# Two decode layers over a cached K and V: the next pair's keys ahead of a pair's values, a shorter row chain, two filler heads

## The chip, the cores and the metric

The kernel runs on one core of one Trainium2 chip (trn2). The metric is the device time of that core in microseconds (us), the median over runs. Three numbers recur, so they get names. The **item** is one of the eight batch rows. **x1** is the moment when an item's first attention is complete and the row chain starts. **Lateness** is how much later than 2.49 us each 1 MB cache load landed after the one before it, summed; 2.49 us is their spacing while the queue is full.

## The reference, cut to what matters

```python
x = A_x                                        # [8, 1, 448]
x = x + A_ref(layernorm(x), k_cache, v_cache, wq, wo)
x = x + B_ref(layernorm(x), w1, w2, w3, w4)
x = x + A_ref(layernorm(x), k_cache, v_cache, wq, wo)   # the same cache again
x = x + B_ref(layernorm(x), w1, w2, w3, w4)

# A_ref: 16 query heads on 8 key/value heads, Sk = 4096, Dh = 256, softmax over Sk, then wo
# B_ref: h = gelu(layernorm(x) @ w1), shifted along a sequence of one token: hs is zero
#        x1 = x + hs;  return x1 + gelu(layernorm(x1) @ w3) @ w4          # F = 1792
```

With one token per sequence, B_ref is two layer norms in a row and one MLP with gelu in its tanh form. Each cache entry is used twice, by layer 1 and by layer 2, and a row's layer 2 can't start before its layer 1 and the row's MLP are done.

## The kernel before

One item has 8 heads in each of 2 layers: 16 **pairs** (a layer and a head). A pair needs 2 MB of keys and 2 MB of values, in four halves of 1 MB. There are 15 half slots in on-chip memory. The keys of five heads (ten halves) and one value half are kept from layer 1 to layer 2; the others are loaded twice. So an item loads 64 - 11 = 53 halves. The keys arrive as rows and are transposed on TensorE (16 transposes per half), copied back by VectorE or ScalarE, and multiplied: per pair 64 small matmuls for the scores, 64 for the values, 20 for the output projection.

The program builds a list of operations with priorities; a planner with assumed durations puts them in a fixed order on each engine.

```python
HALVES = 15; KEEP_K = 5; KEEP_V = 1; REP = 24
...
    def schedule(self):                        # list scheduler, one queue per engine
        ...
            if e == "sp":                      # a DMA issue
                free[e] = t + 0.45
                start = max(t + 1.0, dma_end)  # assumed latency of a load
                dma_end = start + o.dur
            else:
                end = free[e] = t + (o.dur[e] if isinstance(o.dur, dict) else o.dur)
...
    def mlp(src, skey, n, b0):                 # the row chain
        layernorm(src, skey, n, [("full", xnT[:, :, 0:n], "xnT")])
        layernorm(xnT[:, :, 0:n], "xnT", n, [("split", None, None)])
        ...                                    # 56 matmuls, gelu by exp on VectorE and ScalarE, 70 matmuls
...
    def pair(layer, b, h, kept_k, kept_v, keep_k, keep_v):
        for j in range(2):                     # keys: load, transpose, scores
            if ks[j] is None:
                ks[j] = load_half(A_k_cache, b, h, j)
            ...
            for qd in range(2):
                def sc(t, j=j, qd=qd, s_=ks[j]):
                    for s in range(8 * qd, 8 * qd + 8):
                        i = 16 * j + s
                        for c in range(2):
                            a = slot_ap(s_, s * 256, 256)
                            last = t.matmul(ps[:, 2 * i:2 * i + 2 * REP], a[:, c:256:2],
                                            bcast(rhs(c), REP, 1), start=(c == 0), stop=(c == 1))
                    return last
        ...                                    # max over partitions, exp, sum
        for j in range(2):                     # values: load and multiply, at once
            if vs[j] is None:
                vs[j] = load_half(A_v_cache, b, h, j)
            ...                                # 32 matmuls per half, then 20 with wo
...
    for b in range(B):
        if b + 1 < B:
            fill = lambda: layer1(b + 1, free_heads)    # 3 filler heads while the chain runs
        else:
            fill = lambda: layer2(b - 1, free_heads)
        mid(b, l2_heads[0], l2_heads + free_heads)      # x1 -> norms, MLP, norm -> new queries
        fill()
        layer2(b, l2_heads)                             # the five heads with kept keys
        if b != B - 2:
            layer2(b, free_heads)
        if b + 1 < B:
            layer1(b + 1, kept_heads)                   # keeps ten halves of keys again
```

At x1 ten slots hold kept keys and one a kept value half. Only four slots circulate until the row chain has made the new queries.

## Time and profile before

| | before |
|---|---|
| time, median of 3 runs | 1298.9 us (1296.33 to 1300.52) |
| TensorE busy | 1013.1 us, 78% |
| bytes over the load queue | 455.19 MB |
| lateness, mean of seven items | 22.2 us (18.6 to 25.4) |
| x1 to first new query, mean | 31.6 us |
| last cache load landed, then to the end | 1265.6 us, then 34.9 us |

The page of the kernel before: the span, each engine's busy time, then in 40 slices of the span the granted TensorE clock, the DMA share and the GB/s, and last the queues.

```profile
span 1300.5 us, 52136 instructions
PE 1013.1 (78%) x24217; PEld 963.1 (74%) x24217; DVE 523.1 (40%) x1804; ACT 214.4 (16%) x743; POOL 97.7 (8%) x270
...
PEclk8789889988899887998899988999899888997886
...
GB/s 357 413 399 383 276 399 417 417 256 340 409 418 387 262 334 419 416 331 303 370 417 416 284 292 367 417 416 295 315 409 417 405 252 317 413 390 240 371 365 2
...
q1 hardware_dynamic: 68192, 455.19, 89.4%
q8 instruction: 190, 3.11, 1.0%
```

The queue runs at 416 to 418 GB/s and dips eight times, once per item. What SyncE, which issues the loads, waited for (columns: line, what it waited for, us in total, times, longest us):

```profile
SPq L372 <- PE psS L632: 720.3, 201, 10.4
SPq L372 <- PE psS L594: 228.8, 90, 4.7
```

A load waits for a slot, and a slot comes free by the value matmuls (L632) or the score matmuls (L594) that read it. What TensorE waited for, same columns:

```profile
PE psS L632 <- ACT pT L614: 71.4, 77, 1.6
PE psS L594 <- issue: 45.1, 29, 3.9
PE psT L680 <- DMA kv<-in_A_k_cache_dram: 44.3, 19, 4.2
PE psS L632 <- issue: 36.4, 26, 3.3
...
PE psW L655 <- issue: 14.5, 8, 3.3
```

TensorE waited 71.4 us for the softmax of ScalarE (L614) and 44.3 us for keys. The lines with "issue" are time in which it waited for nothing that the profile shows: 102.0 us in 70 pauses over the whole run.

One item's end, in windows of 10 us around x1 = 433.8. Columns: window, busy us (instructions) of PE, PEld, DVE, ACT and POOL after the window's length, granted clock, DMA share, GB/s.

```profile
393.80:403.80 10.00, 8.10 (x182) 7.38 (x181) 4.82 (x12) 1.81 (x7) 0.75 (x2) 1.00 1.01 416
423.80:433.80 10.00, 8.44 (x166) 7.97 (x163) 4.34 (x13) 1.23 (x5) 0.75 (x2) 0.83 0.54 189
433.80:443.80 10.00, 7.19 (x99) 6.89 (x97) 5.33 (x28) 2.40 (x7) 0.75 (x2) 0.67 0.62 211
```

The load queue falls to half at x1. The timeline just before it (start, us, engine, line, operation, and in brackets the idle time and what ended it):

```profile
424.31 0.56 PE L594 MATMUL psS<-q1T,kv 128*128 128x48 bf16 x16 [0.39 <-DVE kv L688]
...
426.52 0.57 PE L632 MATMUL psS<-pT,kv 128*128 128x48 bf16 x16 [1.17 <-ACT pT L614]
...
438.50 1.97 PE L680 MATMUL psT<-ident_f,kv 128*128 128x128 f32 x8 [2.33 <-DMA kv<-in_A_k_cache_dram]
```

The last pair's scores ended at 424.9 and its value matmuls could start only at 426.5, after the softmax, though the values had landed at 419.8. Twelve microseconds later TensorE sat waiting for keys that had been issued late.

### The profile page before, as it was taken

What the parts mean: (1) busy time and instruction counts of PE and PEld (TensorE: products, weight loads), DVE (VectorE), ACT (ScalarE), POOL (GpSimd) and SP (SyncE); (2) the same over time, 40 slices, a digit from 0 to 9 for tenths busy, and PEclk for the clock granted to TensorE, in tenths of its full rate; (3) what the DMA queues carried; (4) which work ended last, traced back from release to release, by engine and by line L of the source; (5) the groups of instructions that cost most, each with busy time, mean ns of one, the idle gap of its engine ahead of it and who ended that gap; (6) DMA issues with size and microseconds to landing.
All of it is one profiled execution on the core that took longest, in us unless ns stands there. A gap on an engine that the chain in (4) does not pass through costs nothing.

```text
span 1300.5 us, 52136 instructions
## 1 busy us (share of the span) xinstructions
PE 1013.1 (78%) x24217; PEld 963.1 (74%) x24217; DVE 523.1 (40%) x1804; ACT 214.4 (16%) x743; POOL 97.7 (8%) x270
## 2 busy tenths in 40 slices
PE   5767868887788787888688787888778878778784
PEld 4766868877687777777677786877767868778774
DVE  2334414453244522446144541445324453344234
ACT  1112102111111111221011110212111111121110
POOL 0000000000000000000100000000010000000100
PEclk8789889988899887998899988999899888997886
DMA  9999799979999799988999789998899978996980
GB/s 357 413 399 383 276 399 417 417 256 340 409 418 387 262 334 419 416 331 303 370 417 416 284 292 367 417 416 295 315 409 417 405 252 317 413 390 240 371 365 2
DMA packets 68408, 458.52 MB, mean 353 GB/s; under 512 B 6992, under 2 KB 13024, under 8 KB 13536
## 3 DMA queue, kind: packets, MB, share of 16 engines
q1 hardware_dynamic: 68192, 455.19, 89.4%
q8 instruction: 190, 3.11, 1.0%
q14 instruction: 26, 0.21, 0.0%
HBM read 455.15 MB, written 0.01 MB: 350 GB/s over the span
## 4 chain that ended last, share of the span: by engine, by line
PE 63%; DMA 14%; issue 10%; DVE 6%; ACT 4%; SPq 2%; POOL 2%
PE psT L680 22%; PE psS L632 17%; PE psS L594 14%; DMA kv<-in_A_k_cache_dram 12%; PE psW L655 5%; ACT pT L614 3%; DMA kv<-in_A_v_cache_dram 3%; DVE kv L688 2%; PE psC L491 2%; SPq L372 2%; POOL gm L606 2%; DVE pm L604 1%; PE psC L541 1%; DVE nb L608 1%; ACT kv L689 0%
## 5 line engine op out<-in xcount | busy, mean ns | idle before, releaser
L680 PE MATMUL psT<-ident_f,kv 128*128 128x128 f32 x2816 | 448.3, 299 | 46.0 <-DMA kv<-in_A_k_cache_dram 44.3
L688 DVE COPY kv<-psT 128x512 f32<-128x512 f32 x483 | 333.0, 690 | 294.6 <-PE psT L680 291.5
L632 PE MATMUL psS<-pT,kv 128*128 128x48 bf16 x8192 | 300.3, 190 | 110.8 <-ACT pT L614 71.4
L632 PEld LDWEIGHTS psS<-pT,kv 128*128 128x128 bf16 x8192 | 277.1, 101 | 132.4 <-ACT pT L614 85.9
L680 PEld LDWEIGHTS psT<-ident_f,kv 128*128 128x128 f32 x2816 | 332.2, 152 | 48.7 <-DMA kv<-in_A_k_cache_dram 46.3
L689 ACT COPY kv<-psT 128x512 f32<-128x512 f32 x221 | 129.4, 586 | 678.7 <-PE psT L680 678.7
L594 PE MATMUL psS<-q2T,kv 128*128 128x48 bf16 x4096 | 149.8, 192 | 48.1 <-issue 42.9
L594 PEld LDWEIGHTS psS<-q2T,kv 128*128 128x128 bf16 x4096 | 136.4, 102 | 51.6 <-issue 46.1
L594 PE MATMUL psS<-q1T,kv 128*128 128x48 bf16 x4096 | 145.7, 184 | 25.6 <-DVE kv L688 17.5
L594 PEld LDWEIGHTS psS<-q1T,kv 128*128 128x128 bf16 x4096 | 126.7, 97 | 38.6 <-issue 27.1
L614 ACT ACTIVATE pT<-psS,nb 128x32 bf16<-128x32 f32 x256 | 72.8, 294 | 372.4 <-DVE nb L608 372.1
L606 POOL PARTITION_ALL_REDUCE gm<-pm x128 | 45.4, 355 | 1050.2 <-DVE pm L604 1027.9
L655 PE MATMUL psW<-oT,wo_sb 128*128 128x24 bf16 x2560 | 89.9, 183 | 18.2 <-issue 14.5
L655 PEld LDWEIGHTS psW<-oT,wo_sb 128*128 128x128 bf16 x2560 | 83.6, 97 | 23.1 <-issue 20.2
L604 DVE TENSOR_REDUCE pm<-psS 128x2 f32<-128x64 f32 x128 | 28.6, 224 | 132.2 <-PE psS L594 131.9
L644 DVE TENSOR_TENSOR oT<-psS,rc 128x4 bf16<-128x4 f32 x128 | 20.2, 158 | 109.8 <-PE psS L632 109.6
L619 POOL PARTITION_ALL_REDUCE Db<-rs x128 | 51.9, 405 | 117.7 <-ACT pT L614 117.7
L614 ACT ACTIVATION_READ_ACCUMULATOR pT<-psS,nb 128x1 f32 x256 | 50.3, 196 | 0.0
L621 DVE RECIPROCAL rc<-Db 128x2 f32<-128x2 f32 x128 | 20.9, 164 | 66.5 <-POOL Db L619 66.5
L491 PE MATMUL psC<-yb,wq_sb 128*128 128x16 bf16 (+1 forms) x864 | 38.6, 175 | 6.8 <-issue 4.4
L608 DVE TENSOR_SCALAR nb<-gm 128x2 f32<-128x2 f32 x128 | 21.6, 169 | 51.4 <-POOL gm L606 50.6
L491 PEld LDWEIGHTS psC<-yb,wq_sb 128*128 128x128 bf16 x864 | 32.9, 97 | 8.6 <-issue 4.8
(77 smaller groups left out, 323.7 us busy)
## 6 DMA issues: line engine op xcount, KB each, us to landing
kv<-in_A_v_cache_dram SPq DMA_DIRECT2D x248, 1024.0 KB, 11.1
kv<-in_A_k_cache_dram SPq DMA_DIRECT2D x176, 1024.0 KB, 16.5
wo_sb<-in_A_wo_dram SPq DMA_DIRECT2D x1, 3584.0 KB, 32.5
wq_sb<-in_A_wq_dram SPq DMA_DIRECT2D x3, 1024.0 KB, 11.3
w_sb<-in_B_w_dram SPq DMA_DIRECT2D x1, 1568.0 KB, 24.1
w_sb<-in_B_w_dram SPq DMA_DIRECT2D x3, 448.0 KB, 26.0
wqx_sb<-in_A_wq_dram SPq DMA_DIRECT2D x2, 256.0 KB, 14.2
w3x_sb<-in_B_w_dram SPq DMA_DIRECT2D x2, 112.0 KB, 20.4
```

Of the source, the lines that this page charges most:

```text
L491: last = t.matmul(psC[:, mt * w_:(mt + 1) * w_], w, r, start=(kc == 0), stop=(kc == 3))
L594: last = t.matmul(ps[:, 2 * i:2 * i + 2 * REP], a[:, c:256:2], bcast(rhs(c), REP, 1), start=(c == 0), stop=(c == 1))
L604: plan.op("dve", lambda v: v.tensor_reduce(pm[nr][:, :], sview, axis=AX.X, op=ALU.max), 0.23, "max", rd=scs, wr=[("pm", nr)], banks=[bk], ...
L606: plan.op("pool", lambda gp: gp.partition_all_reduce(gm[nr][:, :], pm[nr][:, :], P, RO.max), 0.46, "max", rd=[("pm", nr)], wr=[("gm", nr)] ...
L608: plan.op("dve", lambda v: v.tensor_single_scalar(nb[nr][:, :], gm[nr][:, :], -INV_SQRT_DH, ALU.mult), 0.15, "max", rd=[("gm", nr)], wr=[( ...
L614: return a.activation(pT[nr][:, :, :].rearrange("p i j -> p j i")[:, jj, :], sview[:, jj, :], ACT.Exp, bias=nb[nr][:, jj:jj + 1], scale=IN ...
L619: plan.op("pool", lambda gp: gp.partition_all_reduce(Db[nr][:, :], rs[nr][:, :], P, RO.add), 0.5, "sum", rd=[("rs", nr, 0), ("rs", nr, 1)] ...
L632: last = t.matmul(ps[:, PV0 + 2 * REP * c:PV0 + 2 * REP * (c + 1)], slot_ap(s_, s * 256 + c * P, P), bcast(pT[nr][:, i, :], REP, 1), start ...
L655: last = t.matmul(psW[:, mt * YW:(mt + 1) * YW], dup(wo_sb, 2 * (2 * h + j) + c, mt), bcast(oT[nr][:, c, j:j + 1], YW, 1), start=(k == 0), ...
L680: last = t.transpose(psT[bank][:, s * P:(s + 1) * P], src, ident_f[:, :])
L688: return e.tensor_copy(dst, psT[bank][:, :])
L689: return e.copy(dst, psT[bank][:, :])
```

## The change

The intent has four parts. (1) *Lag*: a pair's value half is put off by one pair, so that the next pair's keys are loaded, transposed and scored before this pair's value matmuls, and the softmax is hidden. (2) *Row chain*: the two norms in a row share one mean and one variance, the reciprocal root takes two steps instead of three, gelu uses tanh, masked outputs take one operation instead of three, and residual sums are merged. (3) *Fillers*: two filler heads, two pairs with kept keys, then the third filler. (4) *Planner*: two durations for TensorE's work, the longer one when the planner takes its clock to be low ("a cold clock" in the prediction), and 2.4 us load latency. When the clock is low is the planner's own assumption. The trace of before shows granted clocks of 0.50 and 1.00: 16 small matmuls took 0.67 us from start to start at 0.50 (440.26 to 440.93) and 0.41 us at 1.00 (417.96 to 418.37).

The diff, cut to its core ("..." where cut):

```diff
+RSQRT_STEPS = ((0.703952253, 1.681914091), (0.5, 1.5000003))
+LAG = 1
+NFILL = 2
...
-                start = max(t + 1.0, dma_end)
+                start = max(t + 2.4, dma_end)
...
+                    d = d[0] if warm else d[1]          # planner: short or long duration
...
-    def layernorm(src, skey, n, outs):
+    def norm(src, skey, n, second, x_plus_norm=None):
...
+            dv(lambda v: v.tensor_scalar(var[:, 1, 0:n], psC[:, 8:8 + n], (1.0 + LN_EPS) / D,
+                                         LN_EPS * LN_EPS, ALU.mult, ALU.add),
+               rd=["psC"], wr=["var1"], banks=["C"])       # second norm's variance from the first's
...
-        for _ in range(3):
+        for half, three in RSQRT_STEPS:
...
+            dv(lambda v: v.scalar_tensor_tensor(yb[:, :, 0], xc[:, :, 0], last, mask[:, :],
+                                                ALU.mult, ALU.mult),
+               rd=["xc", "rsy", "mask"], wr=["yb"])
...
-        plan.op("act", lambda a: a.activation(a_, b_, ACT.Exp, scale=-GELU_K2), 0.3, "chain",
+        plan.op("act", lambda a: a.activation(a_, b_, ACT.Tanh), 0.3, "chain",
                 rd=["g2"], wr=["g1"], prio=CH + len(plan.ops))
-        dv(lambda v: v.tensor_single_scalar(a_, a_, 1.0, ALU.add), rd=["g1"], wr=["g1"])
-        dv(lambda v: v.reciprocal(b_, a_), dur=0.13 + 0.008 * m, rd=["g1"], wr=["g2"])
...
+    def flush(n):
+        while len(pend) > n:
+            pend.pop(0)()
...
-        for j in range(2):
-            if vs[j] is None:
-                vs[j] = load_half(A_v_cache, b, h, j)
...
+        def back():                                   # values, wo and the sum of this pair
+            for j in range(2):
+                if vs[j] is None:
+                    vs[j] = load_half(A_v_cache, b, h, j)
...
+        pend.append(back)
+        flush(LAG if lag is None else lag)
...
-        fill()
-        layer2(b, l2_heads)
+            layer1(b + 1, free_heads[:NFILL])
...
+        layer2(b, l2_heads[:2])
+        if b + 1 < B:
+            layer1(b + 1, free_heads[NFILL:])
+        layer2(b, l2_heads[2:])
```

The number of cache loads and of transposes, score and value matmuls is the same in both kernels.

## The prediction

> **What bounds the kernel now.** It streams 455 MB once (page, DMA queues); both kernels issue the same 424 cache loads of 1 MB. With the queue full, windows of 25 us show 416-418 GB/s and loads land 2.49 us apart (landing times): all traffic at 417 GB/s would take about 1092 us of the 1300. TensorE is busy 78%. The missing ~208 us: (a) eight dips, one per batch item, period 154 us; summing how much later than 2.49 us each load landed gives 21-25 us per full period, 165-170 us in all. (b) The tail: the last values land at 1265.6, the end is 1300.5 (35 us). (c) About 8 us at the start.
>
> **Why the dips.** At an item's end ten of 15 half slots hold kept keys and one a kept value, so four circulate. The queue waits nearly only for matmuls that free a slot (values' 720 us, scores' 229 us). TensorE's order puts each pair's value matmuls between the transposes of the next pair's keys: the last pair's values landed at 419.8, but their matmuls ran 426.5-431, after the next keys landed at 422.3. So issue stops, and a load on an empty queue takes 5.2 us to land, 2.7 more than it streams. Then the row chain (x1 to the first new query, 433.2-464.6, 31.5 us; VectorE 0.19 us per small instruction, and matmuls behind waiting transposes) holds the kept keys.
>
> **What the change does.**
> - Next keys before values: in the built order the next pair's transposes precede a pair's values, so TensorE rarely waits on a later load than the slot it should free. At an item's end x1 starts 1-2 us after the last values land, four key loads (10 us) queued behind. I estimate that two thirds to four fifths of the dips goes.
> - Row chain: VectorE falls from 1804 to 1431 instructions (45 of these are evictions moved to ScalarE): ~36 fewer per item x 0.19 = 7 us, and one mean and one variance round trip. Chain: about 20-23 us.
> - Tanh: [...]the built program still has one table load, as the trace before (1.28 us).
> - Planner with 2.4 us load latency and a cold clock: fewer head-of-line waits.
>
> **Sum.** 1092 + start 9 + tail 20 (one norm fewer ~7, no key work after the last values ~8) + dips 8 x 6 = 48: about 1169. Some dips stay: at full clock TensorE's work for fillers and chain about fills the time of their loads (my estimate, from 0.42 us per 16 small matmuls), and the granted clock there fell to 0.5-0.7 ([...]440-444 us shows 0.50).
>
> Predicted 1170 us, 8 in 10 within 1135 to 1215. Faster by over 2%: 0.96; within 2%: 0.03; slower: 0.01.
>
> **What would show it.** Right: same bytes, spacing still 2.49 us; mean near 390 GB/s; late landing per item below 8 us; chain below 24 us; tail below 23 us; one table load; TensorE busy near 85%. Wrong: dips over 12 us an item with the queue waiting on the fillers' scores; low clock after x1; TensorE waiting for keys with values landed.
>
> **What would make it wrong.** One pair of lag takes slots, so steady stretches could starve; TensorE at half clock could become the limit; or the fixed order drifts from the plan.

The trace of before gives: 16 cache loads issued to an empty queue landed after 4.9 to 6.0 us (median 5.3), and VectorE's small instructions start 0.19 us apart where they follow each other (median). The granted clock in 440 to 444 us was 0.50, with TensorE busy for all 4.00 us.

## The result, and the profile after

| | before | after |
|---|---|---|
| time, median of 4 runs each | 1297.85 us | 1241.38 us (1236.75 to 1244.25) |
| ratio, 95% interval | | 0.9559 (0.9525 to 0.9594) |
| TensorE busy | 1013.1 us | 1025.6 us |
| TensorE stopped on "issue" | 102.0 us, 70 times | 147.5 us, 99 times |
| lateness, mean of seven items | 22.2 us | 16.5 us |
| x1 to first new query | 31.6 us | 19.8 us |
| last cache load to the end | 34.9 us | 18.7 us |

A ratio here is the mean time of one kernel's runs over that of the other's runs of the same rounds, so it isn't quite the ratio of the medians. Executions over 1.5% slower than the fastest of the same kernel are left out of the means. The class is faster; the time is 71 us above the predicted one and 26 us above the top of the range.

The page of the kernel after, same lines:

```profile
span 1242.4 us, 51839 instructions
PE 1025.6 (83%) x24271; PEld 975.8 (79%) x24271; DVE 452.0 (36%) x1431; ACT 240.6 (19%) x788; POOL 98.4 (8%) x270
...
PEclk9878888988989987899789977889889898899978
...
GB/s 349 410 399 402 325 404 417 417 295 346 419 416 396 265 377 417 417 399 291 373 417 417 355 263 381 416 417 351 331 399 416 416 297 350 415 414 256 355 417 143
...
q1 hardware_dynamic: 68192, 455.19, 92.2%
q8 instruction: 191, 3.13, 1.0%
```

The same bytes, fewer VectorE instructions, and the eight dips are still there, only less deep. What TensorE and then SyncE waited for:

```profile
PE psS L676 <- issue: 55.8, 35, 2.7
PE psS L637 <- issue: 45.1, 29, 2.9
PE psW L699 <- issue: 27.8, 18, 3.0
...
PE psT L729 <- DMA kv<-in_A_k_cache_dram: 7.0, 5, 4.2
...
PE psS L676 <- ACT pT L657: 1.1, 1, 1.1
```

```profile
SPq L390 <- PE psS L637: 545.2, 165, 10.6
SPq L390 <- PE psS L676: 392.3, 131, 9.5
```

The waits that the lag was made for are gone: softmax 71.4 to 1.1 us, keys 44.3 to 7.0 us. Yet the loads still wait for slots that TensorE frees, and the "issue" pauses grew. Around x1 = 416.7 the windows (columns as before) show TensorE full:

```profile
406.70:416.70 10.00, 9.13 (x256) 8.44 (x255) 3.95 (x11) 1.93 (x7) 0.76 (x2) 1.00 0.75 281
416.70:426.70 10.00, 9.36 (x198) 8.92 (x197) 6.22 (x23) 3.05 (x6) 0.00 (x0) 1.00 0.80 295
426.70:436.70 10.00, 10.00 (x283) 9.94 (x280) 5.25 (x24) 2.96 (x11) 1.51 (x4) 1.00 0.77 244
```

TensorE has no gap to give, at a granted clock of 1.00, while the load queue runs at 244 to 295 GB/s. The weight loads (PEld) are busy for 9.94 of 10 us in the last window and the matmuls for 10.00. Over the whole run PEld is only 79%, and that number doesn't show the pauses of the next part (147.5 us).

### What the pauses on "issue" are

Four pauses in a row of TensorE in the kernel after, in a stretch where pairs with kept keys run:

```profile
766.57 0.65 PE L699 MATMUL psW<-oT,wo_sb 128*128 128x24 bf16 x18 [2.29 <-issue]
...
772.67 0.23 PE L637 MATMUL psS<-q2T,kv 128*128 128x48 bf16 x3 [1.56 <-issue]
...
778.94 0.35 PE L637 MATMUL psS<-q2T,kv 128*128 128x48 bf16 x7 [1.37 <-issue]
...
785.12 0.46 PE L637 MATMUL psS<-q2T,kv 128*128 128x48 bf16 x12 [1.35 <-issue]
```

They end 6.10, 6.27 and 6.18 us apart, in the middle of groups of like matmuls that have nothing to wait for. Counting TensorE's instructions (a matmul and a weight load each count one) and the packets of the instruction queue in the same trace gives:

```
pause ends   instructions since the pause before   last packet of the instruction queue: started, landed
766.57       507                                   764.25  765.23
772.67       255                                   770.10  771.20
778.94       255                                   776.45  777.56
785.12       255                                   782.76  783.90
```

Every packet of that queue has 16,384 bytes. The pauses over 0.5 us, 88 in this trace, come at multiples of about 255 instructions (distances 252 to 256, 505 to 511, 761 to 767 and so on), and nine of ten end 1.25 to 1.58 us after a packet of that queue landed; for moments drawn at random that delay lies between 0.2 and 6.6 us. The packet that ended a pause started between 1.8 us before the pause and 0.3 us after its beginning (nine of ten). From these figures the author infers that TensorE has used up one packet of its own program and waits for the next; the trace has no record of the wait itself. Where two pauses follow each other by one packet, their ends lie 6.2 us apart (median of 45; nine of ten between 5.8 and 8.2). The same holds in all 20 kernels: 6.2 to 6.4 us. It is a pace and not a fixed cost per packet: in u_lag, a run described below, TensorE worked between 3.4 and 5.8 us before such a pause, and the pause filled up the rest, so that the 27 distances scatter by only 0.2 us (standard deviation) where the working times scatter by 0.6.

These pauses are a large cost here: TensorE stopped over 0.5 us at 88 of about 190 packet boundaries, 143.7 us in all.

The changes of the instruction count bear this out. Taking 3,088 of TensorE's instructions away (12.1 times 256; m_chainpe below) took 12 packets off the queue, 191 to 179; adding 2,048 (8 times 256; m_more_b) added 8, 191 to 199.

By this reading TensorE has a second limit beside its busy time in this kernel: by estimate about 256 of its small instructions per 6.2 us, the measured pace of the pauses. From one x1 to the next this kernel's instruction queue moves 23.5 packets (mean of the first six such distances), which is 23.5 x 6.2 = 146 us. The item's loads need 53 x 2.49 = 132 us. The next table has the mean distance of x1 to x1 over the same six.

| kernel | packets in all (page) | packets per item x 6.2 us | distance of x1 to x1 |
|---|---|---|---|
| before | 190 | 147 | 154.6 |
| after | 191 | 146 | 149.3 |
| after, second chip (c_after) | 191 | 146 | 146.6 |

The kernel before was 8 us per item above what its instructions need; the kernel after is 4 us above on one chip and 1 us above on another. The 6.2 us is an estimate of the limit, from the stretches with pauses: 28 of the 190 distances between packets in the kernel after are below 5.5 us, so it isn't a hard floor for each packet. Nor does the table prove much alone, since by this reading packets are fetched as they are used up, and other kernels lie further off (u_lag 152.4 us for 147, m_more_a 152.2 for 148, m_peboth 139.8 for 128). What the trace does show is that TensorE has almost no other idle time: of the 149.3 us per item in the kernel after it is busy for 126.1 and paused on "issue" for 19.7.

### The profile page after: what moved, and what is told of

Its sections match the earlier page's. It is cut to its first block, busy times and chain, and to the rows that moved or that the text cites. A ratio compares the mean times of both kernels' runs of the same rounds, so it can differ in the third digit from the quotient of the medians.

```text
span 1242.4 us, 51839 instructions
## 1 busy us (share of the span) xinstructions
PE 1025.6 (83%) x24271; PEld 975.8 (79%) x24271; DVE 452.0 (36%) x1431; ACT 240.6 (19%) x788; POOL 98.4 (8%) x270
## 4 chain that ended last, share of the span: by engine, by line
PE 74%; issue 12%; DMA 6%; DVE 4%; SPq 3%; POOL 0%; ACT 0%
PE psT L729 26%; PE psS L637 18%; PE psS L676 17%; PE psW L699 7%; DMA kv<-in_A_k_cache_dram 4%; SPq L390 3%; PE psC L534 2%; DMA kv<-in_A_v_cache_dram 2%; PE psC L474 1%; PE psC L580 1%; DVE oT L688 1%; PE psC L556 1%; DVE kv L737 1%; DVE pm L647 0%; DVE rst L491 0%
## 5 line engine op out<-in xcount | busy, mean ns | idle before, releaser
L729 PE MATMUL psT<-ident_f,kv 128*128 128x128 f32 x2816 | 415.1, 298 | 16.3 <-issue 9.1
L737 DVE COPY kv<-psT 128x512 f32<-128x512 f32 x438 | 301.1, 691 | 197.4 <-PE psT L729 194.7
L729 PEld LDWEIGHTS psT<-ident_f,kv 128*128 128x128 f32 x2816 | 342.3, 153 | 19.0 <-issue 10.8
L676 PE MATMUL psS<-pT,kv 128*128 128x48 bf16 x8192 | 281.9, 188 | 65.1 <-issue 55.8
L676 PEld LDWEIGHTS psS<-pT,kv 128*128 128x128 bf16 x8192 | 251.0, 99 | 72.2 <-issue 62.9
L738 ACT COPY kv<-psT 128x512 f32<-128x512 f32 x266 | 156.1, 587 | 582.3 <-PE psT L729 582.3
L637 PE MATMUL psS<-q2T,kv 128*128 128x48 bf16 x4096 | 163.5, 192 | 41.4 <-issue 41.4
L637 PEld LDWEIGHTS psS<-q2T,kv 128*128 128x128 bf16 x4096 | 141.5, 102 | 48.5 <-issue 41.8
L699 PEld LDWEIGHTS psW<-oT,wo_sb 128*128 128x128 bf16 x2560 | 78.5, 98 | 69.0 <-DVE oT L688 37.8
L711 DVE TENSOR_TENSOR acc<-acc,psW 128x5 f32<-128x5 f32 x96 | 15.6, 162 | 62.6 <-PE psW L699 62.5
## 6 DMA issues: line engine op xcount, KB each, us to landing
w3x_sb<-in_B_w_dram SPq DMA_DIRECT2D x2, 112.0 KB, 20.4
```

What stands on the lines that cost most here:

```text
L676: last = t.matmul(ps[:, PV0 + 2 * REP * c:PV0 + 2 * REP * (c + 1)], slot_ap(s_, s * 256 + c * P, P), bcast(pT[nr][:, i, :], REP, 1), start ...
L699: last = t.matmul(psW[:, mt * YW:(mt + 1) * YW], dup(wo_sb, 2 * (2 * h + j) + c, mt), bcast(oT[nr][:, c, j:j + 1], YW, 1), start=(k == 0), ...
L729: last = t.transpose(psT[bank][:, s * P:(s + 1) * P], src, ident_f[:, :])
L737: return e.tensor_copy(dst, psT[bank][:, :])
L738: return e.copy(dst, psT[bank][:, :])
```

## The experiments

Eighteen kernels ran, in five calls. Each call has its own runs of the kernel before; the ratios are to those. For the kernel after the ratios 0.9559 (first chip) and 0.9503 (c_after, another chip) span the uncertainty; "cost" below is the difference to these two, times 1298 us. Every run passed the comparison with the reference, also those that are wrong, so that comparison doesn't prove a result right. Not every time fell into a range that its expectation named: m_halftr, m_slots18 and i_ahead fell between two, m_more_b beyond both, i_var short of its gain, and u_row and the control c_after missed theirs by 2 us.

### Undoing one part at a time

**u_lag**: the lag undone.

```diff
-LAG = 1
+LAG = 0
```

> The changed kernel with the lag undone (a pair's values load before the next pair's keys), all else kept. If the load order is the main source of the 56 us gained, this run goes back to about 1275 to 1290 us with late landings near 21 us per item. If the row chain and the planner made the gain, it stays within 15 us of 1241.

Measured: 1283.97 us, ratio 0.9863 (0.9811 to 0.9915). The lag is worth 39 to 47 us. What TensorE waited for:

```profile
PE psS L676 <- ACT pT L657: 87.2, 80, 1.6
PE psS L676 <- issue: 34.8, 23, 3.0
```

The softmax waits are back, and the pauses on issue fell from 147.5 to 82.7 us in all: while TensorE waits for the softmax, its next instructions arrive, by the reading above; the trace doesn't show that directly. Of the 86 us of softmax waits that the lag takes away, 65 us come back as pauses.

**u_row**: the row chain of before.

```diff
-    def norm(src, skey, n, second, x_plus_norm=None):
+    def layernorm(src, skey, n, outs):
...                                 (norms, gelu, masked outputs and mlp as before)
```

> The old row chain (three norms, exp gelu with reciprocal, copies) in the changed kernel, all else kept. If the length of the row chain sets the dips: chain back to about 30 us, +8 to +10 us per item, 1310 to 1325 us. If the dips are set by TensorE's work in the stage: the chain grows by about 8 us but the time only by the tail's 7 us plus at most 2 us per item, 1248 to 1265 us.

Measured: 1267.2 us, 0.9722 (0.9684 to 0.976); chain 29.1 us, tail 30.1 us, lateness 18.7 us per item, of which 10.7 us lie 35 to 40 us after x1, where the slots are held until the queries exist. The new chain is worth 21 to 28 us, 11 of them in the tail.

**u_fill**: three filler heads in a row.

```diff
-NFILL = 2
+NFILL = 3
```

> Three filler heads again ahead of the first pair on kept keys, all else kept. TensorE-bound theory (the stage after x1 has more matmul work than its loads last): a third filler adds 8 us of matmul work before the kept keys' slots come free, so the stage stays short of slots longer: 5 to 25 us slower than 1241. If the number of fillers does not matter: within 5 us.

Measured: 1250.29 us, 0.9601 (0.9575 to 0.9626): 5 to 13 us, little beyond the difference of two chips.

**u_plan**: the planner's old constants.

```diff
-                start = max(t + 2.4, dma_end)
+                start = max(t + 1.0, dma_end)
-                    d = d[0] if warm else d[1]
+                    d = d[0]
...                                 (two small durations as before)
```

> The planner's old constants (1.0 us to landing, matmuls always at full clock), all else kept. If head-of-line waits from a wrong plan were a large part of the dips before: 1265 to 1285 us, and TensorE waiting on key loads with values landed. If not: within 10 us of 1241.

Measured: 1236.07 us, 0.9509 (0.9458 to 0.9561): the planner's part gave nothing.

The three other parts sum to 65 to 88 us where the whole gave 57 to 64 us, so they overlap.

### Taking work away or adding it

**m_halftr** (wrong): half of the transposes, with the same bytes copied back.

```diff
-            for s in range(4):
+            for s in range(2):
...
+            dst = dst.rearrange("p (a n) -> p a n", a=2)
+            half = bcast(psT[bank][:, 0:256], 2, 1)
```

> Wrong result on purpose: half of the key transposes left out (1408 of 2816), the evictions kept at full size, the order of every engine unchanged. TensorE-bound theory: about 165 us less matmul work, the dips fall from 16-17 us per item to under 6, time 1130 to 1165 us. Slot or latency theory (few slots, 5.2 us from issue to landing on an empty queue): dips stay above 12 us per item, time above 1210 us.

**m_chainpe** (wrong): fewer matmuls in the row chain of a single row, 1 of 4 per sum for the MLP's input and the queries, 3 of 14 for its output.

```diff
-            for kc in range(4):
+            for kc in range(4 if n > 1 else 1):
...
-                for fc in range(14):
+                for fc in range(14 if n > 1 else 3):
```

> Wrong result on purpose: the row chain's large matmuls cut per item (mlp 56 to 14 and 70 to 15, queries 128 to 32, about 5 us of TensorE time per item), order unchanged. TensorE-bound theory: dips shrink by 3 to 5 us per item, 1200 to 1217 us. If TensorE is not what frees slots late: within 8 us of 1241.

Measured: m_halftr 1202.49 us, 0.9236 (0.919 to 0.9282); m_chainpe 1210.41 us, 0.9294 (0.925 to 0.9339). Lateness is 11.6 us per item in both. Pages of m_halftr, then of m_chainpe:

```profile
PE 912.2 (76%) x22863; PEld 836.3 (70%) x22863; DVE 440.0 (37%) x1431; ACT 237.0 (20%) x788; POOL 97.9 (8%) x270
...
q8 instruction: 180, 2.95, 1.0%
```

```profile
PE 980.6 (81%) x22727; PEld 929.7 (77%) x22727; DVE 450.3 (37%) x1431; ACT 240.6 (20%) x788; POOL 97.9 (8%) x270
...
q8 instruction: 179, 2.93, 1.0%
```

These two differ in busy time and hardly in instruction count. Against the control (c_after, 1013.1 us busy), m_halftr takes 101 us of busy time away and m_chainpe 33 us, three times less. Both take 11 to 12 packets away, and both gain nearly the same: 35 to 42 and 27 to 34 us. Over the two, time follows the instructions better than the busy time, but they don't decide it: the busy time would explain m_chainpe's gain as well. Nor does time follow the instructions fully: 11 packets at 6.2 us would be 68 us, and the distance of x1 to x1 is 143.6 us where the packets need 137. In m_halftr the waits of the value matmuls for their loads rose from 7.9 to 29.9 us and those for keys from 7.0 to 17.6, so with less work in the way the loads begin to limit too. The copies back were left at full size, and the scores waited 32.3 us for them (1.0 in the kernel after). The clock fell as well; m_halftr's first 10 us after its x1:

```profile
407.20:417.20 10.00, 9.36 (x214) 8.41 (x214) 6.05 (x24) 3.04 (x6) 0.00 (x0) 0.83 0.75 294
```

TensorE is as busy there as in the kernel after, with less to do, at a granted clock of 0.83 instead of 1.00.

**m_peboth** (wrong): m_halftr and m_chainpe together.

> Wrong result on purpose: half the transposes and most of the row chain's matmuls left out together, order unchanged. Joint limit: the two savings add in the stage after x1, lateness 6 to 9 us per item, 1160 to 1185 us. If slots and landing latency alone set what was left with half the transposes: 1195 to 1203 us as there.

Measured: 1173.42 us, 0.9025 (0.8993 to 0.9056), 167 packets, lateness 7.8 us. That this is close to the predicted 1170 us is chance: it took half of the transposes and most of the chain's matmuls away to get there, about 12% of TensorE's instructions (42,638 against 48,542) and 134 us of its busy time (879.4 against 1013.1 in c_after). Value matmuls now wait 52.6 us for loads, so the loads limit more than before.

**m_chaindve**: ten idle reciprocals in each row chain, on VectorE alone.

```diff
+        def centre(v):
+            if second and n == 1:
+                for i in range(5):
+                    v.reciprocal(junk[i][:, :], ones_f[:, 0:64])
...                                 (five more before the copy of the MLP's first result)
```

> Ten needless VectorE reciprocals per item on the row chain (about 5 us per item longer chain), no matmul added, TensorE's and the queue's order unchanged. TensorE-bound theory: the chain has slack or shifts only, under 2 us per item, below 1258 us. Chain-bound theory: the full 5 us per item, near 1280 us.

Measured: 1273.62 us, 0.9791 (0.9741 to 0.9841), chain 23.7 us. One of the two groups of the added operation in the profile (line, count, busy us, mean ns):

```profile
L572 DVE RECIPROCAL junk<-ones_f 128x64 f32<-128x64 f32 x40 | 17.6, 506 | 8.3 <-PE psC L562 8.3
```

Ten of 506 ns make 5 us per item, 40 us in all, and 30 to 37 us came out at the end. What TensorE waited for in the chain, first here, then in the kernel after:

```profile
PE psC L480 <- DVE sq L474: 14.8, 10, 2.1
PE psC L591 <- DVE hT L582: 11.9, 9, 1.6
```

```profile
PE psC L580 <- DVE hT L571: 1.6, 1, 1.6
PE psC L474 <- DVE sq L468: 1.1, 2, 0.5
```

TensorE's order was fixed without the added work, so TensorE itself stood still for VectorE, 26.7 us in place of 2.7. A longer chain isn't in itself paid in full: in i_big (below) the chain takes about 26 us and the time doesn't grow, and in u_row it takes 9 us more per item, 74 us in all, for 10 to 17 us outside the tail.

**m_keep4**: keys of four heads kept instead of five, so two more circulating slots at x1 and two more loads per item.

```diff
-KEEP_K = 5
+KEEP_K = 4
```

> Four heads' keys kept in place of five: two more free slots after x1 (six for four), two more loads per item (16 MB in all, +40 us at the measured 2.49 us a load) and their transposes. Slot theory: dips fall to under 10 us per item, so the time stays within 15 us of 1241. TensorE-bound theory: transposes are added, dips stay 13 or more, 1265 to 1290 us.

Measured: 1266.75 us, 0.9723 (0.9675 to 0.9771), lateness 13.3 us. Sixteen loads more cost 40 us at 2.49 us each; 21 to 29 us came out. The slots help a little and don't remove the dips.

**m_slots18** (wrong): three more slots, made by letting the MLP read the attention's weights.

```diff
-HALVES = 15
+HALVES = 18
...
+    w3_sb, w3x_sb, w4_sb = wq_sb, wqx_sb, wo_sb
```

> Wrong result on purpose: the mlp reads the query and output weights in place of its own, which are neither loaded nor kept; their memory gives three more half slots (18, so seven in place of four after x1) and 3.2 MB less to load (about 8 us). Joint limit: three loads more can land without the query, so lateness falls by 5 to 7 us per item: 1175 to 1195 us. If TensorE's work alone sets it (it must do the same work per item whatever the slots): 1222 to 1240 us, 8 us for the loads left out and no more.

Measured: 1218.13 us, 0.9373 (0.9334 to 0.9412), lateness 13.3 us. The gain is 17 to 24 us, of which 8 us are the 3.2 MB of weights no longer loaded (at 417 GB/s). The rival theory that too few slots make the dips falls as the main cause: seven circulating slots at x1 instead of four left most of the lateness (16.5 us in the kernel after, 14.2 in c_after).

### Moving work

**c_after**: the kernel after, unchanged, as a control.

> The changed kernel again, as the control of this call: 1236 to 1246 us, dips 16 to 17 us per item.

Measured: 1234.17 us, 0.9503 (0.945 to 0.9557). One of its four runs, 1251.88 us, was 1.6% above the fastest, 1231.62, at a mean granted clock of 0.891 against 0.899, and is left out of the ratio. Lateness is 14.2 us per item, not the expected 16 to 17, and TensorE is busy for 1013.1 us, 12 less than in the profile of the first chip.

**i_big**, **i_ahead**, **i_ahead1**: TensorE's order near x1. In i_big the chain's large matmul groups go behind the fillers' transposes and scores; in i_ahead all fillers' keys go ahead of the whole chain; in i_ahead1 only the first filler's.

```diff
+    def ahead():
+        return 2 * CH + len(plan.ops) if first[0] else None      # i_ahead, i_ahead1
...
-                banks=[("T", bank)])
+                banks=[("T", bank)], prio=ahead())
```

> The planner puts the two fillers' transposes and scores ahead of the row chain's large matmuls (mlp and queries), nothing else changed. Theory now: the scores that free the slots stand behind the row chain in TensorE's one queue, while the chain has some 10 us of slack before the slots run out (in the run with the old row chain, 10.7 us of lateness came only 35 to 40 us after x1). Then late landings between x1 and x1+30 fall from 10.5 to 5 us or less, the chain grows to 22 to 26 us: 1195 to 1220 us. Rival, the sum of TensorE's work in the stage: the order does not matter, 1233 to 1250 us. Second rival, chain length alone: a longer chain costs time, above 1255 us.

> Both fillers' transposes and scores ahead of the whole row chain, so the first new query comes about 30 us after x1. Theory: no lateness between x1 and x1+25, but 5 to 10 us after x1+30, when the slots run out before the query: 1215 to 1250 us, no better than the control or little. Chain length alone: above 1270 us.

> Only the first filler's transposes and scores ahead of the whole row chain. Theory: between the control and the run with the large matmuls behind, 1200 to 1230 us. Rivals: as there.

Measured: i_big 1238.12 us, 0.9542 (0.9491 to 0.9592); i_ahead 1265.41 us, 0.9749 (0.9703 to 0.9794); i_ahead1 1235.04 us, 0.951 (0.9458 to 0.9563). In i_big the lateness moved from the 30 us around x1 to 30 to 40 us after it and kept its size. The theory that the order near x1 makes the dips falls: order moves them, and a bad order adds to them.

**i_var** and **i_varq**: the squares for the variance in bf16, and in i_varq also the other heads' queries put off until after the first pair with kept keys.

```diff
-        dv(lambda v: v.tensor_tensor(sqv, xcv, xcv, ALU.mult), rd=["xc"], wr=["sq"])
+        dv(lambda v: v.tensor_tensor(sqb[:, :, 0:n], xcv, xcv, ALU.mult), rd=["xc"], wr=["sqb"])
```

> Right result: the squares for the variance in bf16[...] (before: eight instructions of about 1.0 us together, twice per item). About 0.8 us off the chain twice per item: at 0.8 us of time per us of chain, 1.2 us per item, 1220 to 1232 us against 1234 to 1241 of the changed kernel.

> Right result: as i_var, and the queries of all heads but the first kept one are made after that head's scores, so 2.9 us of query matmuls leave the way to the first free slots of kept keys. Joint limit: another 1 to 2.5 us per item, 1200 to 1222 us. If not: as i_var.

Measured: 1235.93 us, 0.9517 (0.9481 to 0.9554), and 1236.02 us, 0.9504 (0.9473 to 0.9535). Both are misses: no gain. In hindsight they take 144 of 48,542 TensorE instructions away, half a packet. In the kernel after, the variance's four f32 matmuls appear as eight instructions (1.04 us at 418.6), the four bf16 ones of the mean as four (0.24 us at 416.7); the chain's saving was estimated from the first.

**m_more_a** and **m_more_b**: nearly the same busy time added in two places, about 27 us by plan (by the pages 22 to 24 us over the kernel after, 35 to 36 over c_after). In m_more_a the first filler's transposes run twice, near x1. In m_more_b half the scores of four pairs with kept keys run twice, in the stretch where the queue is full and TensorE looked as if it had slack.

```diff
-                    transpose_piece(ks[j], pc)
+                    transpose_piece(ks[j], pc, 2 if layer == 0 and h == 0 and b else 1)   # m_more_a
...
-                    for s in range(8 * qd, 8 * qd + 8):
+                    twice = layer == 1 and h in l2_heads[1:] and qd == 0                  # m_more_b
+                    for s in list(range(8 * qd, 8 * qd + 8)) * (2 if twice else 1):
```

> Right result: the first filler's transposes are made twice (224 more at 0.12 us, 27 us of TensorE in all, 3.8 us per item in seven items), just after x1. If TensorE's work in that stretch sets the lateness: 18 to 30 us slower than the changed kernel (1252 to 1270 us). If there is slack: under 8 us slower.

> Right result: half the score matmuls of four pairs on kept keys are made twice (1024 more at 0.026 us, 27 us of TensorE in all), in the stretch from about x1+25 where TensorE is 65 to 90% busy. If only the stretch around x1 is bound by TensorE: under 8 us slower (below 1247 us). If the kernel is bound by the sum of TensorE's work wherever it falls: 18 to 30 us slower.

Measured: m_more_a 1261.17 us, 0.9671 (0.9627 to 0.9716); m_more_b 1279.46 us, 0.9802 (0.9754 to 0.9851). Pages of m_more_a, then of m_more_b:

```profile
PE 1049.1 (83%) x24495; PEld 1001.1 (79%) x24495; DVE 451.2 (36%) x1431; ACT 240.6 (19%) x788; POOL 98.5 (8%) x270
...
q8 instruction: 192, 3.15, 1.0%
```

```profile
PE 1047.8 (82%) x25295; PEld 998.1 (78%) x25295; DVE 452.0 (35%) x1431; ACT 240.2 (19%) x788; POOL 97.9 (8%) x270
...
q8 instruction: 199, 3.26, 1.0%
```

The theory that TensorE is short of time only near x1 falls: the same busy time costs 15 to 22 us near x1 and 31 to 39 us in the stretch with "slack". The busy time of the two differs by 1.3 us. What differs, beside the place and the kind of work, is the instructions: 448 more (1.75 packets) in m_more_a, 2,048 more (8 packets) in m_more_b. Eight packets at 6.2 us are 50 us, by estimate. m_more_b's distance of x1 to x1 is 153.2 us, where its 24.5 packets per item need 152; m_more_a's is 152.2, where its 23.8 need 148. The stretch had no slack: by the reading above, TensorE runs in its small matmuls at the rate at which its instructions come. The pair doesn't separate this from the place of the added work.

No run with a right result had a lower ratio than the control c_after, 0.9503.

## Why the prediction was right and where it was wrong

**Right: the mechanism of the gain.** The order of loads is the main part, 39 to 47 us when undone alone. The softmax and key waits went from 115.7 to 8.1 us.

**Right: the chain, the tail and the bytes.** The chain was predicted at about 20 to 23 us and measured 19.8; the tail was predicted at 20 and measured 18.7; bytes and the spacing of 2.49 us are the same.

**Right: tanh needs no second table.** Both traces have one table load, of 1283 ns, the one before with exp alone and the one after with exp and tanh.

**Wrong: "dips 8 x 6 = 48".** This is the term that failed. The prediction estimated that two thirds to four fifths of the dips would go; about a quarter went (22.2 to 16.5 us per item; 14.2 in c_after). Its own sign for this came out: dips over 12 us an item, with the queue waiting longer on scores (545.2 us, before 228.8). Lateness was 16.5 us per item in the mean of seven and 18.0 in the last: 16.5 x 7 + 18.0 = 133.5, and 138 over all loads. Lateness of 138 and a tail of 18.7 leave about 1086 of the 1242 us for streaming. Against the prediction's sum the lateness is 90 us over its term; streaming with the start is 15 us under (1092 + 9 were allowed) and the tail 1 us under, which leaves 73 us.

**The step behind it: "TensorE is busy 78%".** The prediction gave TensorE no term of its own in the sum, and expected that the value matmuls would follow their loads once the order was right. It didn't add the pauses that stood in the same profile: 1013 us busy and 102 us of "issue" are 1115 us of the 1300 before the change. When the lag took the softmax waits away, part of that time came back as more pauses (102.0 to 147.5 us), since TensorE then, by the reading above, ran into the end of its delivered instructions more often (88 pauses over 0.5 us, 61 before). After the change busy and pauses make 1173 of 1242 us. That TensorE's time is the limit is shown by experiment: less work on it shrank lateness and time (m_chainpe, m_halftr, m_peboth), and more work on it cost time in both places (m_more_a, m_more_b). How much of the limit the pauses make is read from the traces. A check was possible with the trace of before, where pauses that follow each other also end 6.2 us apart (median of 41): 189 distances of 6.2 us, 25.8 us until the first packet of the instruction queue and 9 us after the last make 1207 us. That is an estimate with the measured pace, and 1170 lies well below it.

**How this makes a dip at x1.** In the kernel after, the time from a key load's landing to the end of its last transpose is 15.9 us at 50 us after x1 and 8.5 us just before the next x1 (mean of six items): TensorE comes out of the pairs with kept keys behind the loads and catches up slowly. While slots are plenty, the queue stays full and this doesn't show. When keys are being kept and only four slots circulate, each late matmul delays a load. In m_more_b the first number is 20.4 us. The pauses themselves don't fall into the dip: of 19.7 us per item only 0.5 lie in the first 20 us after x1, where TensorE is full of work, and 12.3 lie 20 to 70 us after it. So they can act on the dip only through what they leave behind, such as this backlog. That is read from the traces; no run changed the backlog alone.

**Also wrong: the clock as the cause.** The prediction feared half clock after x1, since the trace of before has a granted clock of 0.50 there (440 to 444 us). What makes the clock fall isn't shown here. In the windows shown above the clock there is 1.00 with TensorE full. Not every item is like this: in the first 10 us after x1 the granted clock of the eight items is 0.66 to 1.00, 0.90 in the mean. But in c_after it is 1.00 there in all eight, and 14.2 us of lateness per item remain, so half clock isn't what makes the dips. A part may be the clock's: between the two chips' profiles the mean clock differs (0.888 and 0.899), the busy time of TensorE by 12.5 us and the span by 12.6.

**What stays open.** That the pauses are waits for instructions is read from 20 traces, by their period, the packets and their timing; no run changed the supply alone, for instance by moving the same work with larger matmuls. Why a packet takes 6.2 us isn't settled: that it waits behind the cache loads is a guess that no trace here shows, since in stretches without full load too few pauses follow each other to tell. And why taking 11 packets away gave 35 to 42 us and not 68 is only partly seen, in the waits for loads and copies and the lower clock.

## What to carry to other kernels

Add an engine's pauses on "issue" to its busy time before you call the rest room (here 147.5 to 1025.6 us of 1242), and look whether they come at a steady count of instructions, as here at multiples of about 255 among small matmuls: then the count of instructions may be a limit of its own beside the busy time. When a change takes a wait away, ask what the engine will meet next; here 65 of 86 us of hidden softmax waits came back as pauses. Add the same work in the stretch that you believe has slack: it tells more than taking work away where you believe it is scarce.
